# Own halves of two blocks ahead of swapped halves, an earlier norm, and a batch's loads written later, in a fused attention and feed-forward kernel

## Chip, cores and metric

The kernel runs on one NeuronCore of a Trainium2 chip. The metric is the time of one execution on the device, in microseconds (us). Profiles are of one execution each; their spans are about 2 us shorter than the times, which are taken around the whole execution.

## The reference

Attention with squared ReLU in place of softmax, then a gated feed-forward on its output:

```python
# q, k, v: (8 batches, 12 heads, 448 rows, 64)    x: (3584, 768)    d_ff = 1536
scores = q @ k.T / sqrt(64)
attn   = maximum(scores, 0) ** 2 / 448
x      = concat_heads(attn @ v)
xn     = x / sqrt(mean(x * x, -1) + 1e-6) * rms_g
out    = (silu(xn @ w_gate) * (xn @ w_val)) @ w_out
```

## The kernel before

The kernel goes through the eight batches. While TensorE computes the feed-forward of batch b, scores and values of batch b+1 are woven in. Everything stays transposed: `xT` holds 768 model columns as six tiles of 128 partitions. Gate and value weights lie in one tile, `wgv_sb`: gate rows in partitions 0 to 63, value rows in 64 to 127. A matmul with 64 rows of contraction for the gate and one for the value then run side by side in the two halves of the array (in the trace such a pair starts 0.01 us apart, at 99.36 and 99.37 us). For that, each of them needs every 64-row half of x once in its own partitions: half of x is there (`xT`, the *own* halves), the other half has to be moved across by a DMA into `xD`, the *swapped* halves:

```python
def swap(b, j0, j1, eng=None):
    for hf in (0, 1):
        (eng or nc.sync).dma_start(
            out=xDs[b][hf * HALF : (hf + 1) * HALF, j0:j1, :],
            in_=xTs[b][(1 - hf) * HALF : (2 - hf) * HALF, j0:j1, :])

def norm_apply(b):
    ...
    for kt in range(KT):                       # KT = 6
        nc.vector.tensor_tensor(out=xTs[b][:, kt, :], in0=src[:, kt, :],
                                in1=rstds[b][:], op=ALU.mult)
        if kt % 3 == 2:
            swap(b, kt - 2, kt + 1)            # four DMAs in all, of 168 KB each

def rounds(b, fb, parts, r0, r1, x=None):      # rounds 0..5 own, 6..11 swapped
    for r in range(r0, r1):
        kt, own = r % KT, r < KT
        src = (x or (xTs[b], xDs[b]))[0 if own else 1]
        ...                                    # one matmul for gate, one for value

def block_first(b, fb):                        # 12 matmuls, own halves
    gvs[b, fb] = [ps_m.tile([P, S], FP32, name=nm, tag="mm")[:] for nm in ("psG", "psV")]
    rounds(b, fb, gvs[b, fb], 0, KT)

def block_second(b, fb):                       # 12 matmuls, swapped halves; silu; product
    ...

def gate_value(b, f0=0):
    units = []
    for fb in range(f0, FT):                   # FT = 12 blocks
        units.append(lambda fb=fb: block_first(b, fb))
        units.append(lambda fb=fb: block_second(b, fb))
    return units
```

The first three blocks of batch 0 are computed from the x before its norm (`raw_x`) and scaled afterwards, so that TensorE has work while the norm is made. `steps` are pieces of batch 1's attention.

```python
raw_x = xTs[0], xDs[0]
blocks = [early_block(0)]
rounds(0, 0, blocks[0], 0, KT, raw_x)          # block 0, own
norm_stat(0)                                   # sum of squares, sqrt, reciprocal
steps.pop(0)()
rounds(0, 0, blocks[0], KT, 2 * KT, raw_x)     # block 0, swapped
early_out(0, 0, blocks[0])
norm_apply(0)
for fb in range(1, EB):                        # blocks 1 and 2 likewise
    ...
```

The loads run on GpSimd's queue, which also converts float32 to bf16 on the way. In the first 62 us it issues q, k, v of batches 0 and 1 among the weights, then q, k, v of batch 2. The rest of the batches:

```python
fetch(3)                                       # q, k, v of batch 3
weave(out_tiles(0, 0, full), [(1, lambda: norm_stat(1)), (1, lambda: norm_apply(1))])
for b in range(1, B):
    main = gate_value(b)
    ...                                        # output tiles, attention of b + 1 as sides
    if b + 2 < B:
        sides += [(12, lambda b=b: trans_fill(b + 2, 0)), (NB + 2, lambda b=b: trans_fill(b + 2, 1))]
        if b + 3 < B:
            sides += [(NB + 2, lambda b=b: fetch(b + 3))]
    weave(main, sides)                         # (position, f): f is called before unit number position
```

## Time and profile before

| | before |
|---|---|
| median time | 473.26 us (three runs, 470.99 to 474.21); 472.41 with the run beside the change |
| TensorE busy | 450.9 of 470.2 us |
| waits of TensorE for xD | 6.9 us, in two places but for 0.3 us in the last batch |
| clock at one half | about 3.4 us in each of the two places |

In the profile's lines PE is TensorE, PEld its weight loads, DVE VectorE, ACT ScalarE, POOL GpSimd and SP SyncE; a q behind a name is that engine's queue, L424 a line of the kernel. Tiles named ps lie in PSUM, the memory that TensorE writes its sums to. Four rows of the profile's page of the kernel before: the first is the engines' busy time, the others are tenths over 40 equal slices of the span (9 is 90% or more): TensorE's busy share, its granted clock (9 is 0.9 or more of full speed), the DMA engines' busy share.

```profile
...
PE 450.9 (96%) x4748; PEld 252.0 (54%) x4748; DVE 265.8 (57%) x311; ACT 280.0 (60%) x415; POOL 53.6 (11%) x79
...
PE   6997899979999999999999999999999999999995
...
PEclk9798999998999999999999999999999999999998
DMA  9999999991401899039941999039931810041013
...
```

TensorE is full nearly everywhere; apart from the start and the end it falls short most in slice 4 (35 to 47 us, place 1 from here on) and slice 9 (94 to 106 us, place 2). The waits of TensorE in the kernel before (who waited for whom: us in total, times, longest) say for what:

```profile
...
PE psE L424 <- DMA xD<-xT: 2.8, 4, 1.4
PE psG L424 <- DMA xD<-xT: 2.3, 1, 2.3
PE psV L424 <- DMA xD<-xT: 1.8, 4, 0.7
...
```

The swapped halves. `psE` are the early blocks of batch 0; `psG` and `psV` are the gate and value sums of the regular blocks. Windows of the kernel before: stretch in us, its length, busy us of PE, PEld (weight loads), DVE, ACT, POOL with the count of instructions, granted clock (1.00 is full), DMA share as the profile counts it (it can pass 1), GB/s.

```profile
...
36.00:44.00 8.00, 5.19 (x47) 2.35 (x44) 5.12 (x6) 4.04 (x7) 2.41 (x5) 1.00 1.42 208
44.00:48.00 4.00, 4.00 (x28) 2.07 (x26) 2.19 (x5) 2.20 (x4) 0.69 (x1) 0.57 1.53 198
48.00:54.00 6.00, 5.30 (x64) 2.65 (x62) 3.13 (x3) 3.96 (x7) 1.41 (x2) 1.00 1.29 216
...
98.00:102.00 4.00, 2.86 (x40) 1.85 (x37) 0.09 (x1) 1.88 (x3) 0.00 (x0) 1.00 1.29 193
102.00:106.00 4.00, 1.93 (x11) 0.70 (x12) 0.00 (x0) 0.00 (x0) 0.00 (x0) 0.94 1.13 311
106.00:110.00 4.00, 4.00 (x30) 1.97 (x26) 1.72 (x2) 2.01 (x3) 0.00 (x0) 0.63 0.37 139
143.00:197.00 54.00, 54.00 (x586) 30.64 (x584) 32.18 (x37) 34.51 (x51) 4.97 (x7) 1.00 0.71 120
...
```

The two places look alike. TensorE idles (5.2 of 8 us busy at 36 to 44; 2.9 and 1.9 of 4 us at 98 to 106), and just after, the clock is cut: 0.57 in 44 to 48, 0.63 in 106 to 110 (in windows of 0.1 us it is 0.5 from 44.1 to 47.5 and from 105.5 to 108.9 us). The last line is a stretch of the later batches: full and at clock 1.00.

The chain of work that ended last (followed back from the last instruction, at each step to what released it), in the kernel before (start, us, what), has the swap three times:

```profile
...
45.67 8.20 DMA xD<-xT
...
98.62 6.83 DMA xD<-xT
...
420.51 3.07 DMA xD<-xT
...
```

The first ends at 53.87 us, the second at 105.45 us. The third is the same swap in the last batch, where no load runs: 3 us. What runs beside the second are the loads of batch 3, in GpSimd's timeline of the kernel before (start, duration of the issue, what, and in brackets the idle time before and its releaser):

```profile
...
86.68 0.99 POOL L95 DMA_DIRECT2D qb<-in_q_dram  x1
91.24 0.96 POOL L95 DMA_DIRECT2D kb<-in_k_dram  x1 [3.58 <-issue]
92.19 0.94 POOL L95 DMA_DIRECT2D vb<-in_v_dram  x1
...
```

### The profile page before, as it was taken

To read this page: it belongs to the slowest core of one execution; us is meant where nothing else is said; L and a number is where in the kernel's file an instruction comes from. 1 tells how busy PE (TensorE), PEld (TensorE's weight loads), DVE (VectorE), ACT (ScalarE), POOL (GpSimd) and SP (SyncE) were. 2 spreads that over 40 slices of the span, in tenths; PEclk is the share of its full clock that TensorE was granted. 3 is DMA by queue.
4 is the path that set the end of the run, shared out by engine and by line. 5 is a ranking of instruction groups with operands and counts; after the bars stand their busy time and mean duration, and the time that the engine had idled before them with its cause. 6 is when DMAs were issued, how large, how long until landed. Compare 5 with 4: busy or idle time off the path is not lost.

```text
span 470.2 us, 10856 instructions
## 1 busy us (share of the span) xinstructions
PE 450.9 (96%) x4748; PEld 252.0 (54%) x4748; DVE 265.8 (57%) x311; ACT 280.0 (60%) x415; POOL 53.6 (11%) x79
## 2 busy tenths in 40 slices
PE   6997899979999999999999999999999999999995
PEld 2343455545556555565556555565556555565563
DVE  2886586536674467577664467576654466552210
ACT  3695677626766567566756567576756567552221
POOL 8333210400000300003000300003000000000000
PEclk9798999998999999999999999999999999999998
DMA  9999999991401899039941999039931810041013
GB/s 102 195 206 204 211 205 178 186 226 56 89 1 33 201 177 140 3 90 186 171 70 36 207 180 127 0 96 186 169 65 36 196 54 1 1 102 60 1 35 102
DMA packets 86799, 53.89 MB, mean 115 GB/s; under 512 B 36576, under 2 KB 80352, under 8 KB 86752
## 3 DMA queue, kind: packets, MB, share of 16 engines
q0 software_dynamic: 44944, 27.73, 41.6%
q1 hardware_dynamic: 41808, 25.47, 26.5%
q8 instruction: 37, 0.61, 0.5%
q14 instruction: 10, 0.08, 0.1%
HBM read 47.19 MB, written 11.01 MB: 124 GB/s over the span
## 4 chain that ended last, share of the span: by engine, by line
PE 83%; DVE 5%; DMA 5%; ACT 4%; issue 1%; POOL 1%; SPq 0%; POOLq 0%
PE psG L424 32%; PE psO L380 20%; PE psV L424 10%; PE psAV L263 9%; PE psS L218 6%; DMA xD<-xT 4%; DVE xT L404 2%; DVE rstd L394 2%; PE psSS L380 1%; PE psW L544 1%; PE psS L177 1%; DMA kb<-in_k_dram 1%; PE psT L134 1%; ACT r L207 1%; ACT r L187 1%
## 5 line engine op out<-in xcount | busy, mean ns | idle before, releaser
L424 PEld LDWEIGHTS <-wgv_sb 64*128 64x128 bf16 x2304 | 124.9, 95 | 104.3 <-issue 19.0
L424 PE MATMUL psG<-xD,wgv_sb 64*128 64x448 bf16 x558 | 121.9, 350 | 2.4 <-DMA xD<-xT 2.3
L424 PE MATMUL psV<-xD,wgv_sb 64*128 64x448 bf16 x558 | 121.6, 350 | 1.8 <-DMA xD<-xT 1.8
L424 PE MATMUL psG<-xT,wgv_sb 64*128 64x448 bf16 x558 | 121.8, 352 | 0.0
L424 PE MATMUL psV<-xT,wgv_sb 64*128 64x448 bf16 x558 | 121.6, 351 | 0.0
L470 DVE TENSOR_TENSOR hT<-sil,psV 128x448 bf16<-128x448 bf16 x93 | 57.7, 620 | 109.8 <-ACT sil L468 109.1
L380 PE MATMUL psO<-wo_sb,hT 128*64 128x512 bf16 (+1 forms) x1344 | 113.6, 326 | 0.0
L232 ACT ACTIVATE r<-psS 112x896 bf16<-112x896 f32 x108 | 96.2, 917 | 22.9 <-PE psS L218 22.8
L380 PEld LDWEIGHTS <-hT 128*64 128x64 bf16 x1344 | 73.9, 110 | 37.2 <-issue 4.1
L468 ACT ACTIVATE sil<-psG 128x448 bf16<-128x448 f32 x93 | 50.7, 545 | 65.3 <-PE psV L424 36.9
L236 DVE TENSOR_TENSOR r<-r 112x1792 bf16<-112x1792 bf16 x72 | 78.4, 1090 | 12.7 <-ACT r L232 11.7
L485 ACT COPY ost<-psO 128x512 f32<-128x512 f32 (+1 forms) x56 | 26.8, 478 | 50.2 <-PE psO L380 44.0
L218 PE MATMUL psS<-qT,kT 64*128 64x448 bf16 (+1 forms) x288 | 48.5, 353 | 0.4 <-DVE r L230 0.4
L394 DVE RECIPROCAL rstd<-rstd 128x448 f32<-128x448 f32 x8 | 23.6, 2953 | 42.2 <-ACT rstd L390 42.2
L279 ACT ACTIVATE xT<-psAV,ga_sb 128x448 bf16<-128x448 f32 x48 | 28.2, 631 | 25.9 <-PE psAV L263 25.9
L230 DVE TENSOR_SCALAR r<-psS 112x896 bf16<-112x896 f32 x36 | 39.1, 1085 | 5.3 <-PE psS L218 5.3
L263 PE MATMUL psAV<-r,vb 112*64 112x448 bf16 x384 | 41.8, 358 | 0.2 <-ACT r L207 0.2
L165 POOL DMA_DIRECT2D qT<-qT x12 | 6.5, 539 | 280.1 <-DMA qT<-qb 155.6
L263 PEld LDWEIGHTS <-vb 112*64 112x64 bf16 x384 | 20.0, 110 | 20.5 <-issue 9.3
L218 PEld LDWEIGHTS <-kT 64*128 64x128 bf16 (+1 forms) x288 | 17.6, 97 | 19.6 <-issue 8.5
L404 DVE TENSOR_TENSOR xT<-xT,rstd 128x448 bf16<-128x448 bf16 x48 | 26.4, 620 | 0.3
L246 DVE TENSOR_TENSOR r<-r 112x1792 bf16<-112x1792 bf16 x23 | 24.5, 1086 | 0.1
(50 smaller groups left out, 248.6 us busy)
## 6 DMA issues: line engine op xcount, KB each, us to landing
xD<-xT SPq DMA_DIRECT2D x32, 168.0 KB, 2.9
vb<-in_v_dram POOLq DMA_DIRECT2D x7, 672.0 KB, 19.0
qb<-in_q_dram POOLq DMA_DIRECT2D x6, 672.0 KB, 12.4
kb<-in_k_dram POOLq DMA_DIRECT2D x6, 672.0 KB, 15.0
qT<-qT POOLq DMA_DIRECT2D x24, 168.0 KB, 4.1
out_dram<-ost SPq DMA_DIRECT2D x8, 336.0 KB, 4.7
wgv_sb<-in_moe_w_gate_dram POOLq DMA_DIRECT2D x6, 384.0 KB, 16.5
wgv_sb<-in_moe_w_val_dram POOLq DMA_DIRECT2D x6, 384.0 KB, 16.7
```

Source lines behind the costliest of these rows:

```text
L218: nc.tensor.matmul(out=psS[: end - o, hf, :S], lhsT=flat[prt, o:end], rhs=qT[prt, 1 - hf : 3 - hf, h % HH], start=True, stop=True,)
L230: nc.vector.tensor_relu(out=r[:, cp], in_=src)
L232: nc.scalar.activation(out=r[:, cp], in_=src, func=ACT.Relu)
L236: nc.vector.tensor_tensor(out=r[:], in0=r[:], in1=r[:], op=ALU.mult)
L263: nc.tensor.matmul(out=part[hh * D : (hh + 1) * D, :], lhsT=ld["v", b][:, 2 * j + hh, c * D : (c + 1) * D], rhs=rsq[b, 2 * j + hh, c], sta ...
L279: nc.scalar.mul(out=xTs[b][:, j, :], in_=psAV[:, i, :], mul=ga_sb[:, j : j + 1])
L380: nc.tensor.matmul(out=ps[prt, :w], lhsT=lhsT[:, prt], rhs=rhs, start=start, stop=stop)
L394: nc.vector.reciprocal(out=rstd[:], in_=rstd[:])
L404: nc.vector.tensor_tensor(out=xTs[b][:, kt, :], in0=src[:, kt, :], in1=rstds[b][:], op=ALU.mult)
L424: nc.tensor.matmul(out=parts[part][:, :S], lhsT=wgv_sb[prt, h, fb * P : (fb + 1) * P], rhs=src[prt, kt, :], start=(r == 0), stop=(r == 2 * ...
L468: nc.scalar.activation(out=s[:], in_=psG, func=ACT.Silu)
L470: nc.vector.tensor_tensor(out=hT[:, fb, o : o + S], in0=s[:], in1=psV, op=ALU.mult)
```

## The change

The intent is to have work for TensorE that needs no swapped half while the swaps are under way, to norm batch 1 earlier, and to have the loads of batch b+2 issued in the course of batch b's feed-forward rather than beside its swap.

```diff
 def gate_value(b, f0=0):
     ...
+    if b < B:
+        units[1], units[2] = units[2], units[1]      # first, first, second, second
     return units
 ...
-    blocks = [early_block(0)]
-    rounds(0, 0, blocks[0], 0, KT, raw_x)
+    blocks = [early_block(fb) for fb in range(2)]
+    near, far = KT + 4, 2 * KT
+    rounds(0, 0, blocks[0], 0, KT, raw_x)
     norm_stat(0)
-    steps.pop(0)()
-    rounds(0, 0, blocks[0], KT, 2 * KT, raw_x)
-    early_out(0, 0, blocks[0])
+    rounds(0, 1, blocks[1], 0, KT, raw_x)
+    for fb in range(2):
+        steps.pop(0)()
+        rounds(0, fb, blocks[fb], KT, near, raw_x)
     norm_apply(0)
-    for fb in range(1, EB):
+    for fb in range(2):
+        rounds(0, fb, blocks[fb], near, far, raw_x)
+        early_out(0, fb, blocks[fb])
+    for fb in range(2, EB):
     ...
-    sides += along(0, len(main) / len(steps), steps)
+    sides += along(0, (len(main) - 1) / len(steps), steps)   # batch 1's last values one unit earlier
 ...
-fetch(3)
-weave(out_tiles(0, 0, full), [(1, lambda: norm_stat(1)), (1, lambda: norm_apply(1))])
+weave(out_tiles(0, 0, full), [(0, lambda: norm_stat(1)), (0, lambda: norm_apply(1))])
 for b in range(1, B):
     ...
     if b + 2 < B:
-        sides += [(12, lambda b=b: trans_fill(b + 2, 0)), (NB + 2, lambda b=b: trans_fill(b + 2, 1))]
-        if b + 3 < B:
-            sides += [(NB + 2, lambda b=b: fetch(b + 3))]
+        sides += [(2, lambda b=b: fetch(b + 2))]
+        sides += [(13, lambda b=b: trans_fill(b + 2, 0)), (NB + 3, lambda b=b: trans_fill(b + 2, 1))]
```

More of the change, by code (lines that the diff above doesn't have):

```diff
@@ L584 @@
         raw_x = xTs[0], xDs[0]
-        blocks = [early_block(0)]
+        blocks = [early_block(fb) for fb in range(2)]
+        near, far = KT + 4, 2 * KT
         rounds(0, 0, blocks[0], 0, KT, raw_x)
         norm_stat(0)
-        steps.pop(0)()
-        rounds(0, 0, blocks[0], KT, 2 * KT, raw_x)
-        early_out(0, 0, blocks[0])
+        rounds(0, 1, blocks[1], 0, KT, raw_x)
+        for fb in range(2):
+            steps.pop(0)()
+            rounds(0, fb, blocks[fb], KT, near, raw_x)
         norm_apply(0)
-        for fb in range(1, EB):
+        for fb in range(2):
+            rounds(0, fb, blocks[fb], near, far, raw_x)
+            early_out(0, fb, blocks[fb])
+        for fb in range(2, EB):
             blocks.append(early_block(fb))
-            steps.pop(0)()
-            rounds(0, fb, blocks[fb], 0, KT, raw_x)
-            steps.pop(0)()
-            rounds(0, fb, blocks[fb], KT, 2 * KT, raw_x)
+            for r0 in range(0, far, KT):
+                steps.pop(0)()
+                rounds(0, fb, blocks[fb], r0, r0 + KT, raw_x)
             early_out(0, fb, blocks[fb])
```

## The prediction

> **What bounds it now.** TensorE: busy 450.9 of 470.2 us (page, part 1); from 110 to 408 us it is 98 to 100% busy at clock 1.00 (windows) and waits 0.7 us in all after 110 us (view of waits). Loads that move there change nothing. The change can earn only where TensorE starves for swapped halves (xD):
>
> 1. First blocks, 39 to 54 us. It waits 2.8 us for xD of the raw x, then 0.7 us for xD of the normed x, which lands at 53.87 us (chain). In one-us windows the clock is 0.5 from about 44.4 to 47.7 us: matmuls take 577 instead of 350 ns, some 1.7 us lost.
> 2. Start of batch 1. It waits 2.3 + 0.6 + 0.2 us for xD between 100.9 and 105.5 us; then the clock is 0.5 to 108.8 us, another 1.7 us. The swap's last part took 6.8 us to land (chain), against 3.1 us at the same place of the last batch, where no loads run. Here the loads of batch 3 (three of 672 KB, issued 86.7 to 92.2 us) keep the DMA engines busy.
>
> The Trainium skill, "TensorE: Matmul & The Clock Gate", Part 1, states half rate after an idle window of about 3.4 us; the trace agrees: both slow stretches last about 3.4 us and follow mostly idle ones.
>
> **What the change does.** The matmul counts stay equal. It
> - runs own halves of two blocks, at every batch's start, before a swapped half: 12 matmuls, 1.15 us, more cover;
> - issues the loads of batch b+2 after batch b's swap;
> - runs batch 1's norm before the first output tile (2.6 us) instead of after it.
>
> **Costed.**
> - Place 2: the norm starts earlier, the swap should land in about 3 us, 1.15 us more cover: xD lands about 2 us before it is wanted. Wait (3.1 us) and slow clock (1.7 us) go: -4.8 us. Nearly certain. The last batch's 0.3 us goes too.
> - Place 1: the raw waits are better covered, but norm, multiplies and swap keep their times, so the normed xD still lands near 53.9 us behind the weight loads. TensorE arrives earlier and waits longer. What is kept is the work done meanwhile: one own half and a score pair, 1.35 us. The slow clock at 44 us hid behind this same barrier; the longer wait (about 50.5 to 53.9 us) may bring it back after 54 us, where it costs: expected +0.8 us.
> - Small costs: squares before batch 1's last values (0.3 us), its norm sum waiting for ScalarE (0.2 us), PSUM buffers held by two blocks at batch starts (0.3 us).
>
> Sum: -4.8 - 0.3 - 1.35 + 0.8 + 0.8 = -4.9 us.
>
> **Predicted: 468.4 us** (-1.0%), 8 in 10 between 465.0 and 471.5. Faster by over 2%: 0.06; within 2%: 0.92; slower: 0.02.
>
> **What would show it.** Right: no wait for xD and clock 1.00 near 98 to 110 us, xD landing in about 3 us there; TensorE still waiting for xD up to about 54 us (1 to 3 us in all); stage times from 110 us on unchanged (52.7 us per batch). Wrong: if the normed xD lands well before 53 us or its waits vanish, I gain 2 us more; a slow stretch after 54 us costs 1.7; new waits of psG or psV for ScalarE or VectorE at each batch's third block would mean the PSUM cost is larger.
>
> **What would make it wrong.** The phase of the clock's window differs from run to run; before's spread (3.2 us) is two thirds of the gain; weights may delay the swap otherwise than traced.

## The result

The changed kernel takes 467.24 us (median of four runs, 467.19 to 467.56), the kernel before in the same rounds 472.41 us (470.99 to 474.21). The ratio is 0.989, 95% interval 0.985 to 0.993. Here and below a ratio is the mean time of one kernel's fast runs over that of the other's in the same rounds, so it is not quite the ratio of the medians. Executions over 1.5% slower than the fastest of the same kernel are left out of the means.

The same rows of the page, of the changed kernel:

```profile
...
PE 448.1 (96%) x4748; PEld 250.0 (54%) x4748; DVE 264.5 (57%) x311; ACT 279.2 (60%) x415; POOL 53.6 (12%) x79
...
PE   6999799989999999999999999999999999999995
...
PEclk9799999999999999999999999999999999999999
DMA  8999999994302997059922999059921810041013
...
```

TensorE's busy time fell by 2.8 us with the same matmuls; two slow stretches of 1.7 us each are gone from this profile. The span fell by 5.0 us. The waits of TensorE for xD in the changed kernel, first in the window 36 to 62 us and then in 96 to 112 us:

```profile
...
PE psV L424 <- DMA xD<-xT: 1.1, 2, 0.7
PE psG L424 <- DMA xD<-xT: 0.8, 2, 0.5
PE psE L424 <- DMA xD<-xT: 0.6, 1, 0.6
...
```

```profile
...
PE psV L424 <- DMA xD<-xT: 2.1, 2, 1.8
```

They fell from 6.9 to 4.6 us; the 0.3 us of the last batch are gone. The windows of the changed kernel:

```profile
...
36.00:44.00 8.00, 7.24 (x72) 3.52 (x69) 5.04 (x5) 5.27 (x9) 2.39 (x4) 1.00 1.42 209
44.00:48.00 4.00, 4.00 (x55) 2.23 (x53) 4.00 (x6) 2.99 (x5) 0.84 (x2) 1.00 1.42 214
48.00:54.00 6.00, 3.98 (x32) 1.62 (x29) 3.31 (x4) 3.12 (x5) 0.97 (x2) 1.00 1.32 225
...
98.00:102.00 4.00, 3.04 (x31) 1.38 (x30) 0.00 (x0) 2.21 (x3) 0.00 (x0) 1.00 1.26 232
102.00:106.00 4.00, 2.83 (x27) 1.44 (x27) 0.75 (x2) 1.33 (x3) 0.00 (x0) 1.00 1.19 310
106.00:110.00 4.00, 4.00 (x45) 2.71 (x43) 3.89 (x5) 3.34 (x6) 0.00 (x0) 1.00 0.74 129
...
```

The clock is 1.00 throughout this profile (its mean over the span is 0.992; the other three runs have 0.986, 0.987 and 0.992, and no profile shows where the two lower ones lost it). The dip of place 1 has moved from 36–44 to 48–54 us. In place 2 TensorE still waits 2.1 us. And this is the surprise: the chain and GpSimd's timeline of the changed kernel show the swap of batch 1 and the loads of batch 3 as follows.

```profile
...
95.81 8.23 DMA xD<-xT
...
```

```profile
...
85.37 0.97 POOL L95 DMA_DIRECT2D qb<-in_q_dram  x1
92.27 0.95 POOL L95 DMA_DIRECT2D kb<-in_k_dram  x1 [5.92 <-issue]
93.21 0.93 POOL L95 DMA_DIRECT2D vb<-in_v_dram  x1
...
```

The swap takes 8.2 us, not 3, and the loads of batch 3 are still issued at 85 to 93 us. They have not moved: the swap was issued 2.8 us earlier and landed only 1.4 us earlier.

### Where the 5.0 us are

Marks in the two profiles, at points that come after the same work:

| mark | before | after | gained so far |
|---|---|---|---|
| output tiles of batch 0 and norm sum of batch 1 begin | 86.43 | 84.95 | 1.5 us |
| norm sum of batch 2 begins | 145.51 | 141.10 | 4.4 us |
| norm sum of batch 7 begins | 410.91 | 406.28 | 4.6 us |
| end of the span | 470.2 | 465.2 | 5.0 us |

Place 1 gave 1.5 us and place 2 gave 2.9 us. The 4.4 us at the second mark can be put together from place 2 alone, because TensorE stands there until the swap has landed, however early it came. The swap ends at 104.04 us (95.81 + 8.23) instead of 105.45 us (98.62 + 6.83): 1.4 us. Ahead of it TensorE has now done one own half more and a pair of scores: 1.15 + 0.2 us. And the clock is no longer halved after it: 1.7 us. Sum 4.45 us, measured 4.4. So the 1.5 us of place 1 count in the end only in so far as they let the norm, and with it the swap, start sooner.

### The profile page after: what moved, and what is told of

It reads as the page before. It is cut to its first block, busy times and chain, and to the rows that moved or that the text cites. A ratio compares the mean times of both kernels' runs of the same rounds, so it can differ in the third digit from the quotient of the medians.

```text
span 465.2 us, 10855 instructions
## 1 busy us (share of the span) xinstructions
PE 448.1 (96%) x4748; PEld 250.0 (54%) x4748; DVE 264.5 (57%) x311; ACT 279.2 (60%) x415; POOL 53.6 (12%) x79
## 4 chain that ended last, share of the span: by engine, by line
PE 76%; DMA 18%; SPq 2%; POOL 1%; DVE 1%; issue 0%; ACT 0%; POOLq 0%
PE psG L424 33%; PE psO L380 21%; PE psV L424 7%; PE psS L218 6%; PE psAV L263 6%; DMA wgv_sb<-in_moe_w_gate_dram 6%; DMA wgv_sb<-in_moe_w_val_dram 5%; DMA kb<-in_k_dram 4%; DMA kT<-kb 2%; DMA xD<-xT 2%; PE psSS L380 1%; SPq L157 1%; DVE xT L404 1%; POOL kb L95 0%; POOL qb L95 0%
## 5 line engine op out<-in xcount | busy, mean ns | idle before, releaser
L424 PEld LDWEIGHTS <-wgv_sb 64*128 64x128 bf16 x2304 | 121.6, 94 | 102.1 <-issue 15.2
L380 PEld LDWEIGHTS <-hT 128*64 128x64 bf16 x1344 | 74.9, 110 | 36.2 <-issue 4.1
L218 PE MATMUL psS<-qT,kT 64*128 64x448 bf16 (+1 forms) x288 | 47.1, 351 | 0.4 <-DVE r L230 0.4
```

The source lines that it names most:

```text
L218: nc.tensor.matmul(out=psS[: end - o, hf, :S], lhsT=flat[prt, o:end], rhs=qT[prt, 1 - hf : 3 - hf, h % HH], start=True, stop=True,)
L380: nc.tensor.matmul(out=ps[prt, :w], lhsT=lhsT[:, prt], rhs=rhs, start=start, stop=stop)
L424: nc.tensor.matmul(out=parts[part][:, :S], lhsT=wgv_sb[prt, h, fb * P : (fb + 1) * P], rhs=src[prt, kt, :], start=(r == 0), stop=(r == 2 * ...
```

## The experiments

All twelve runs gave correct results. Each kernel was timed in five rounds against the kernel before, on the same chip: x1 to x4 on one, x5 to x8 on a second, x5b and x9 to x11 on a third. "Gate" means this: before some loads, GpSimd copies one column of a tile that is written at the wanted time, so that its queue must wait.

```python
def after(src):
    t = const.tile([P, 1], BF16, name="gate", tag="gate", bufs=2)
    nc.gpsimd.tensor_copy(out=t[:], in_=src)
```

| run | against before | ratio (95%) | median (range), us | swap of batch 1, us | TensorE's wait for it, us |
|---|---|---|---|---|---|
| the change | all | 0.989 (0.985–0.993) | 467.2 (467.2–467.6) | 8.5 | 2.1 |
| x1 | loads moved only | 0.9991 (0.9961–1.0022) | 471.7 (470.0–473.7) | 7.2 | 3.3 |
| x2 | own pair at each batch only | 0.9925 (0.989–0.9961) | 468.7 (466.8–471.6) | 8.0 | 3.0 |
| x3 | earlier norm of batch 1 only | 0.9949 (0.9919–0.9979) | 469.6 (468.9–471.1) | 7.1 | 1.3 |
| x4 | order of first blocks only | 0.9982 (0.9951–1.0013) | 471.4 (470.1–473.9) | 6.3 | 2.2 |
| x6 | loads of batch 3 gated, nothing else | 0.9891 (0.9863–0.9919) | 466.7 (465.7–467.2) | 2.8 | 0 |
| x5b | the change and this gate | 0.9885 (0.9851–0.9919) | 466.0 (463.7–466.8) | 3.1 | 0 |
| x7 | the change and two gates | 0.9829 (0.9795–0.9863) | 463.4 (461.6–465.8) | 7.8 | 1.1 |
| x11 | before and the two gates | 0.9844 (0.9812–0.9877) | 463.5 (462.9–464.9) | 2.9 | 0.3 |
| x10 | x7, batch 2 loaded ahead of output weights | 0.9961 (0.993–0.9992) | 469.1 (468.7–470.2) | 3.9 | 0 |
| x8 | filler matmuls in the waits | 0.9973 (0.9945–1.0001) | 469.8 (469.7–471.8) | 6.6 | 0.7 |
| x9 | the change, old order of first blocks | 0.9911 (0.9874–0.9947) | 467.2 (465.5–468.6) | 6.3 | 0 |

The swap's time is the median of its four DMAs, from issue to landing. x5 is told in the text. Swap, waits and clock are from one profiled run each.

### x1: the moved loads alone

```diff
-fetch(3)
 ...
-        sides += [(12, ...trans_fill(b + 2, 0)), (NB + 2, ...trans_fill(b + 2, 1))]
-        if b + 3 < B:
-            sides += [(NB + 2, lambda b=b: fetch(b + 3))]
+        sides += [(2, lambda b=b: fetch(b + 2))]
+        sides += [(13, ...trans_fill(b + 2, 0)), (NB + 3, ...trans_fill(b + 2, 1))]
```

> Before with only the moved loads (and transposes) of the change. The instruction listing of every engine is the same as of before. Theory A (the record): the loads of batch 3 now start after batch 1's swap, the swap lands in about 3 us, the 3.1 us wait and the 1.7 us of slow clock at the start of batch 1 go: ratio 0.990. Rival B: the place in the program moves nothing, since GpSimd issues a load as soon as its own buffers are free, and nothing makes it wait for TensorE; loads of batch 3 are still issued at 85 to 95 us, the swap still takes 6 to 8 us: ratio 1.000 within 0.003.

Ratio 0.9991, interval 0.9961 to 1.0022. The DMA issues in the window 90 to 110 us of this kernel (what, queue, count, KB each, median us to landing):

```profile
...
xD<-xT SPq DMA_DIRECT2D x4, 168.0 KB, 7.2
...
```

The rival holds. The loads of batch 3 are issued at 85.98, 91.28 and 92.23 us. Listed engine by engine, this kernel is the same program as the one before. The place at which a load is written orders it only against the other instructions of its own queue, and on GpSimd's queue nothing stood between the old place and the new one. GpSimd issues the load when its buffers are free and earlier loads have landed (in the kernel before, kb of batch 3 stood 3.6 us for the transpose that still read its buffer), long before TensorE comes to the unit beside which it is written.

### x2, x3, x4: the other parts, one at a time

x2 swaps `units[1]` and `units[2]` and no more. x3 has the changed `along(...)` and positions 0 in place of 1 for batch 1's norm. x4 has the new order of the first three blocks.

> Before with only the two own halves ahead of the first swapped half at each batch. Theory A (the record) gives it 1.15 us of cover at the start of batch 1 and the 0.7 us of wait before 53.9 us: -1 to -2 us, the slow clock after 105 us staying. Rival B: the cover shortens the idle stretch enough for the clock to stay whole, so -3 to -3.7 us. If PSUM buffers held by two blocks cost 0.3 us a batch, 2 us of that is lost and waits of psG or psV for ScalarE or VectorE show from 110 us on.

> Before with only batch 1's norm and last values moved ahead of the first output tile. Theory A: the norm starts about 1.3 us earlier relative to the output tiles, so the wait at the start of batch 1 falls from 3.1 to about 1.5 us, the clock may stay slow: -1.3 to -2 us. Rival B: without the wait growing to 2 us the clock stays whole as well: -3 us or more.

> Before with only the new order of the first three blocks. Theory A (the record): normed xD still lands near 53 us and holds TensorE there, so almost nothing is kept: 0 to -0.7 us; TensorE waits 3 us or more between 49 and 54 us, and the slow clock of 44 to 48 us may come back after 54 us, which would make it 1 to 2 us slower. Rival B: the time saved at 39 to 48 us is kept: -3 us.

x2 is 0.75% faster (3.5 us), though its profiled run, the slowest of its six, still had both slow stretches (clock 0.50 in 44 to 48 and 0.57 in 106 to 110 us). It spreads over 5 us. That fits gains from cover with a clock that falls in some runs: the mean clock is 0.980 in the slowest run and 0.991 in the fastest, but 0.980 and 0.988 also occur at 469.1 and 470.1 us, and only one run has a profile, so this stays an inference. The PSUM cost did not show: past 112 us no psG or psV waits for ScalarE or VectorE. x3 is 0.5% faster (2.4 us): the wait in place 2 fell from 3.2 to 1.3 us, and the clock was 1.00 in both places of its profile. Its changed spacing also reaches into the first blocks, whose waits were different, so it is not a pure test of place 2. x4 gains nothing that five rounds can see (0.9982, interval up to 1.0013). Its windows show why:

```profile
...
48.00:54.00 6.00, 2.26 (x15) 0.89 (x14) 0.85 (x1) 0.92 (x1) 1.21 (x2) 0.94 1.31 210
54.00:58.00 4.00, 4.00 (x30) 2.11 (x27) 3.40 (x4) 2.73 (x4) 1.66 (x2) 0.66 1.38 201
...
```

TensorE comes sooner to the normed xD and waits longer there (2.26 of 6 us busy), and then it runs at a cut clock, 0.66 in 54 to 58 us. This is what the prediction feared for place 1. The three parts alone add up to 1.4%, together they give 1.1%: they partly pay for the same waits.

### x6: a real delay of batch 3's loads, nothing else

```diff
-fetch(3)
+# batch 1, before unit 3: copy a column of its first hidden block on GpSimd, then fetch(3)
+def fetch_late(b):
+    hT, o = hidden(b)
+    after(hT[:, 0, o : o + 1])
+    fetch(b + 2)
```

> Before, with nothing but the loads of batch 3 made to start after batch 1's first hidden block. This is what the record thought the moved lines would do. Contention theory: the swap lands in 3 to 4 us, so xD is there at about 101.5 us, the wait falls from 3.1 us to under 1 us and the clock stays whole: -3 to -4.5 us, ratio 0.991 to 0.994. Rival (the swap is slow by itself): ratio 1.000.

GpSimd's timeline of this kernel has the gate and the loads behind it; below it are the swap's line in the DMA issues of 90 to 110 us, and the windows of place 2.

```profile
...
103.79 0.19 POOL L419 COPY gate<-hT 128x1 bf16<-128x1 bf16 x1 [17.96 <-DVE hT L480]
104.34 0.97 POOL L95 DMA_DIRECT2D qb<-in_q_dram  x1 [0.36 <-DMA out_dram<-ost]
105.40 0.95 POOL L95 DMA_DIRECT2D kb<-in_k_dram  x1
106.34 0.93 POOL L95 DMA_DIRECT2D vb<-in_v_dram  x1
...
```

```profile
...
xD<-xT SPq DMA_DIRECT2D x4, 168.0 KB, 2.8
...
```

```profile
...
98.00:102.00 4.00, 3.95 (x51) 2.37 (x49) 0.35 (x1) 1.76 (x3) 0.00 (x0) 1.00 0.92 225
102.00:106.00 4.00, 4.00 (x44) 2.41 (x45) 1.96 (x3) 3.21 (x6) 1.76 (x3) 1.00 0.75 236
106.00:110.00 4.00, 4.00 (x44) 2.20 (x42) 3.68 (x5) 2.91 (x4) 1.28 (x2) 1.00 1.19 146
...
```

The loads now start at 104 us, the swap lands in 2.8 us, TensorE never waits for it and the clock stays at 1.00 in place 2 (in place 1 it was still cut, from 43.0 to 46.2 us). The ratio is 0.9891: this one dependence gains as much as the whole change, with TensorE's order of the kernel before, and more than the 3 to 4.5 us that I expected. From the norm sum of batch 1 to that of batch 2 it takes 51.0 us in place of 56.5: 5.5 us, where the prediction had 4.8 us for place 2. The contention theory of the prediction is right. What was wrong was to think that the diff removed the contention.

The Trainium skill, "DMA: Bandwidth & Descriptors", section "Issuing engines are not separate DMA queues", states that DMAs of all issuing engines run on the same 16 DMA engines and interleave. The traces agree: batch 1's swap, issued by SyncE, takes 2.8 us with no load beside it (x6) and 6.3 to 8.5 us beside loads that GpSimd issued.

### x5 and x5b: the gate on the changed kernel

```diff
-        sides += [(2, lambda b=b: fetch(b + 2))]
+        sides += [(3.1, lambda b=b: fetch_late(b) if b == 1 else fetch(b + 2))]
```

> The changed kernel, with the loads of batch 3 made to start late: GpSimd first copies one column of batch 1's first hidden block, so it must wait for that block. If contention of these loads with the swap is what made the swap take 6.8 to 8.5 us (as the record has it), the swap now lands in about 3 us, TensorE's wait at the start of batch 1 (2.1 us in the changed kernel) is gone, and the time is 2 us below the changed kernel: about 465 us, ratio 0.985 to before. Rival: the swap is slow for the sake of the output stores and its own size; then it still takes over 6 us and the ratio stays at 0.989.

> The changed kernel with the late loads of batch 3 once more, since the profiled run of the first try was 2.5 times as long as its other five and tells nothing. Contention theory: swap in about 3 us, no wait for xD between 96 and 112 us, ratio 0.986 to 0.988, about 1 to 2 us below the changed kernel.

The profiled run of x5 took 1171 us; its five others took 464.1 to 466.7 us (ratio 0.987, interval 0.984 to 0.99). In the long run the matmuls took about twice as long each, and TensorE was busy for 1161.2 us in place of 450.9. The group of the swapped value matmuls in it (count | busy us, mean ns | idle before):

```profile
...
L434 PE MATMUL psV<-xD,wgv_sb 64*128 64x448 bf16 x558 | 311.5, 754 | 0.0
...
```

The mean is 754 ns where before has 350 ns, at a recorded clock of 1.00. It did not happen again in any other run, and why it happened is open. x5b is the same kernel once more: swap 3.1 us, no wait in place 2, ratio 0.9885, median 466.0 us. The clear gain over the changed kernel that I expected (1 to 2 us) is not resolved: the intervals overlap. Its profile also had this in place 1:

```profile
...
48.00:54.00 6.00, 3.56 (x26) 1.28 (x22) 2.95 (x3) 2.50 (x4) 1.24 (x2) 0.93 1.33 220
54.00:58.00 4.00, 4.00 (x43) 2.08 (x42) 3.40 (x5) 2.45 (x5) 1.69 (x3) 0.68 1.24 207
...
```

The clock fell after the wait for the normed xD here, while in the profile of the changed kernel, with the same order on TensorE, it did not. So it is not safe that the new order of the first blocks keeps the clock whole.

### x7, x10, x11: the weights too

```diff
-for s in range(4, NSL): fetch_gv(s)            # written at the start of the kernel
-for s in range(FT // 2): fetch_o(s)
 ...
 norm_apply(0)
+after(xDs[0][:, KT - 1, 0:1])                  # wait for batch 0's normed swap
+for s in range(4, NSL): fetch_gv(s)
+for s in range(FT // 2): fetch_o(s)
```

x7 is x5 with this, x11 is x6 with this.

> The kernel of the run before last, and also the last third of the gate and value weights and all output weights made to wait for the first batch's normed swap. If the weight loads are what holds that swap for 8 us, it now lands at about 48.5 us instead of 53 us, TensorE no longer waits for it (1.9 us in the changed kernel), and the time falls by another 1.5 to 2 us: about 463 us, ratio 0.981. Rival: the weights then come too late for blocks 8 to 11 or for the loads of batch 2, new waits appear between 60 and 110 us, and it is no faster than without this part, or slower.

> Before with both loads late and TensorE's order untouched. If all that holds TensorE in these two places is loads in the way of the swaps, this takes most of the gain of the same two gates on the changed kernel (0.983). If the new order is needed as well, because in the old order TensorE meets the raw swap with nothing else to do (2.8 us and a slow clock), then this stays near the late loads of batch 3 alone: 0.987 to 0.990.

In x7 the normed swap is through at 49 us (GpSimd's gate copy runs at 49.06 us), the waits of place 1 are 1.1 us in place of 2.5, and the ratio is 0.9829: 463.4 us, the fastest kernel here by its median. The batch 2 transposes come later in turn and lie beside the swap of batch 1, which took 7.8 us again; 1.1 us of wait came back. x11 leaves TensorE's order as it was and reaches 0.9844. Waits of TensorE for xD in x11, window 36 to 62 us:

```profile
...
PE psE L434 <- DMA xD<-xT: 2.3, 4, 0.9
...
```

What is left in place 1 is the wait for the raw swap; the one for the normed swap is gone. The first theory held: two dependences on GpSimd's queue, without any new order on TensorE, gain at least as much as the change. That they gain more (0.9844 against 0.989) is likely and not certain, since the two were measured on different chips and the intervals overlap; on one chip and in the same rounds, all six times of x11 (462.9 to 464.9 us) lie below all six of x9 (465.5 to 468.6 us), the change with the old order of the first blocks. Whether the new order adds anything on top (0.9829 against 0.9844, measured on different chips, intervals overlapping) is not settled.

x10 was to remove the wait that came back in x7:

```diff
     fetch_gv(s)
+fetch(2)
 for s in range(FT // 2): fetch_o(s)
```

> The kernel with both loads late, and the loads of batch 2 put ahead of the output weights. In the run without this the transposes of batch 2 ended only at about 91 us and the swap of batch 1 beside them took 7.8 us; TensorE waited 1.1 us. Theory: the transposes now end before 84 us, the swap takes about 3 us, the wait goes: 1 us less, about 462.3 us, ratio 0.980. Rival: the output weights come too late for the first output tile (needed at about 83 us) and a new wait for them shows: slower.

The rival won. The swap is quick (3.9 us), but the transposes were still issued only by 93 us, and TensorE now waits for the output weights; after that wait its clock is 0.50 from about 90 to 96.6 us. From the waits of x10 in 62 to 96 us:

```profile
...
PE psO L380 <- DMA wo_sb<-in_moe_w_out_dram: 5.2, 3, 1.9
...
```

The time is 469.1 us. In the page's row of the kernel before, the DMA engines are 90% busy or more until about 106 us, so what is loaded earlier there pushes something else back.

### x8: filler matmuls in the waits

```diff
-rounds(0, 0, blocks[0], KT, 2 * KT, raw_x)
+rounds(0, 0, blocks[0], KT, KT + 4, raw_x)
+warm(7)                                        # matmuls of zeros into a spare PSUM tile
+rounds(0, 0, blocks[0], KT + 4, 2 * KT, raw_x)
 ...
+    if b == 1:
+        sides += [(1, lambda: warm(12))]       # between own and swapped half of the first block
```

> Before, with 7 and 12 useless matmuls (0.19 us each) put where TensorE waits for the swap, at 39 us and at 101 us; nothing else. The swaps land when they did, so the waits' ends stay. If the idle stretches are what halves the clock, it stays whole at 105 us and the 1.7 us there come back: -1 to -2 us in the mean and a smaller spread of the times than before's 470 to 474 us. Rival: the clock falls for another reason (or costs nothing): no change, or slower by what the filler overruns (up to 0.5 us).

Windows of place 2 in this kernel:

```profile
...
102.00:106.00 4.00, 3.70 (x24) 1.41 (x19) 0.00 (x0) 0.92 (x1) 0.00 (x0) 1.00 1.17 264
106.00:110.00 4.00, 3.50 (x36) 1.94 (x36) 1.72 (x2) 2.15 (x3) 0.00 (x0) 1.00 0.65 255
...
```

The useless matmuls fill the wait, the clock stays at 1.00, and from the norm sum of batch 1 to that of batch 2 it takes 54.7 us instead of 56.5 us: 1.8 us, the price of the slow clock alone, since the swap is as slow as ever (6.6 us). In place 1 the normed swap happened to land at 55.4 us in the profiled run, 1.5 us later than in the profile of before, and cost this back. The ratio, 0.9973 (interval up to 1.0001), cannot be told from 1 with certainty; four of its six times are 469.7 to 469.8 us, below every one of before's in the same rounds (470.2 to 474.1).

The Trainium skill, "TensorE: Matmul & The Clock Gate", Part 1, gives the cause as a monitor that halves the clock after an idle window of about 3.4 us. The slow stretches of 3.4 us in the kernel before fit this, those of 6.6 us in place 1 of x2 (41.8 to 48.4 us) and x9 (42.4 to 49.0 us) are twice as long, and in the profile of x8 there is none in place 2 with busy-work in the wait.

### x9: the change without the new order of the first blocks

The edit puts the old `blocks` section back into the changed kernel.

> The changed kernel with the old order of the first three blocks (the new own pair at each batch, the earlier norm and the moved loads stay). If the new order of the first blocks earns nothing of its own, as its run alone (0.998) suggests, this is as fast as the changed kernel: ratio 0.989 to 0.991. If it is what keeps the clock whole in the first blocks when the own pair covers the normed swap, this is 1 to 2 us slower, 0.992 to 0.993, and its times spread over 3 us or more where those of the changed kernel spread over 0.4 us.

The ratio is 0.9911 against 0.989, the median is the same 467.2 us, and the times spread over 3.1 us. The profile had the slow clock in the first blocks:

```profile
...
44.00:48.00 4.00, 4.00 (x24) 1.93 (x22) 3.02 (x5) 2.18 (x4) 0.87 (x2) 0.50 1.46 197
...
```

The wider spread fits the second expectation and the mean cannot tell the two apart. The share of the new order of the first blocks stays open: x4 puts it at about 0.9 us and x9 at about 1.0 us, and neither can be told from nothing. In place 2 this profile shows no wait at all although the swap took 6.3 us: from the norm on it has the changed kernel's order, so the added own half and the earlier norm cover a swap of 6.3 us, and not the 8.5 us of the changed kernel's profile.

## Why the prediction was right, and where not

The time was predicted as 468.4 us and measured as 467.2 us. The sum came out right, but one of its steps was wrong, and errors of opposite sign hid that.

- **"From 110 to 408 us ... Loads that move there change nothing."** The stretch from the norm sum of batch 2 to that of batch 7 took 265.4 us before and 265.2 us after, so nothing changed there. It was no test of moved loads, since no load moved (x1).
- **"Issues the loads of batch b+2 after batch b's swap" and "the swap should land in about 3 us".** This step failed. The loads were still issued at 85 to 93 us, and the swap took 8.2 us. x1 shows that these lines of the diff change nothing (0.9991); x6 shows what they would have done with a dependence (swap 2.8 us, no wait, 0.9891). The sign to read was there before any run: the order of instructions on GpSimd's queue is the same in both kernels, and no new wait stands in it.
- **"Wait (3.1 us) and slow clock (1.7 us) go: -4.8 us."** Half right. The stretch of place 2 gained 2.9 us. The wait fell only to 2.1 us; the clock stayed whole in the profiled run. What is left to do it is the earlier norm and the added own half, which each gain alone (x3: 0.9949, x2: 0.9925).
- **"The last batch's 0.3 us goes too."** Right.
- **"The normed xD still lands near 53.9 us ... TensorE arrives earlier and waits longer. What is kept ... 1.35 us."** Nearly right: it landed about 1 us sooner. TensorE waited for it up to 52.9 us, for 1.9 us in place of 0.7, and 1.5 us were kept at the start of the output tiles.
- **"The slow clock ... may bring it back after 54 us ... expected +0.8 us."** It did not come in the changed kernel's profile; it did in x4 and x5b. As a chance it was right, as a term of this profile it was 0.
- **Small costs, 0.8 us.** Too large. The norm sum of batch 1 was stretched by 0.15 us (1.45 against 1.30 us), batch 1's last values waited for nothing, and no psG or psV waited for ScalarE or VectorE.

So the terms for place 2 were 1.9 us too favourable, and those for the slow clock and the small costs together some 1.5 us too unfavourable. They nearly cancel, so that the sum came out right is in part luck.

## What to carry to other kernels

Moving a load in the program text moves it only against its own queue; to keep it out of the way of a small urgent transfer it needs something to wait for, here a one-column copy of a tile written at the right time. Look at what a DMA-bound wait shares its engines with before giving TensorE more cover: here one such dependence gained as much as the whole change, and two probably more. A wait that holds TensorE until a fixed moment swallows what is gained ahead of it, except for work that would have come after it.

## What the Trainium skill lacked or had wrong

- "TensorE: Matmul & The Clock Gate" speaks of an idle window, and of a kernel in which short idle gaps made the clock go up and down, and gives no measure for a partly idle window. I took the 3.4 us in which TensorE was least busy, for the two places of each profile. The clock was cut wherever TensorE was busy for 1.05 us of them or less (0.92 and 0.49 us in the kernel before) and nowhere with 1.54 us or more. Between, it was cut in some (1.36 us in x9, 1.46 us in x6) and not in others (1.14 us in x11, 1.28 us in the changed kernel), so no threshold follows.
- The same page warns that the clock events of traces have been seen to be unreliable on trn2. It has no case of a whole run in which matmuls take twice their time (754 instead of 350 ns) at a recorded clock of 1.00, as in one run of x5. No run explains it.
- "DMA: Bandwidth & Descriptors" states that DMAs interleave on shared engines but gives no figure for what a small transfer loses beside a backlog of loads: the four DMAs of batch 1's swap, 168 KB each from SBUF to SBUF, landed in 2.8 us with no load beside them and in 6.3 to 8.5 us beside loads.
- No page that I used says that the place of a load in the program text has no effect on its time as long as its own queue has nothing to wait for; x1 measures this as 0.9991 (0.9961 to 1.0022).
